# One decode head's attention output: 64 one-column matmuls replaced by 16 wide ones, placed ahead of the V transposes

## The chip, the cores and the metric

The kernel runs on one core of a Trainium2 chip. The metric is the device time of one execution in microseconds (us), the median of several; the profile is of one execution, and its span (first to last instruction) is a little shorter than the device time.

The engines are named as the profile names them: PE is TensorE (matmuls; PEld is its weight loads), DVE is VectorE, ACT is ScalarE, SP is the engine that issues the transfers (DMA).

## The reference

Attention of one query row per head, forward and backward, with B = 1, H = 32 heads, S = 8192 keys, D = 128, all bfloat16:

```python
def _fwd_reference(q, k, v):
    scale = q.shape[-1] ** -0.5
    scores = jnp.einsum('bhqd,bhkd->bhqk', q, k) * scale
    attn = _softmax(scores, axis=-1)
    return jnp.einsum('bhqk,bhkd->bhqd', attn, v)
...
    _out, _vjp = jax.vjp(_f, q, k, v)
    _grads = _vjp(grad_out)
    _out0 = jnp.asarray(_out)
    return (_out0, *[jnp.asarray(_g) for _g in _grads])
```

In the terms of the kernel, for each head, with p the softmax of the scaled scores and do the incoming gradient:

- O = sum over keys of p times the row of V (the output, out_0)
- dV = p times do, an outer product of 8192 x 128 (out_3)
- dp = V times do, and pdt = O times do, one number
- ds = p times (dp - pdt) times the scale
- dQ = sum over keys of ds times the row of K (out_1), and dK = ds times q, an outer product of 8192 x 128 (out_2)

## The kernel before

Each head's K and V are 2 MB each and lie in on-chip memory as [128 partitions, 64 slots, 128], so a partition holds 64 consecutive keys. K has three buffers, V has two, and each of the two outer products has two (`gpool`). Heads go one after another in a written order: a manual schedule, so every engine runs its instructions in the order of the program text, and the program text interleaves head h with the rest of head h - 1.

For one head h the order is:

1. `k_blocks`: VectorE transposes K in 32 x 32 blocks. `k_scores` (L153): 64 matmuls of four columns with the transposed K as weights give the scores. `s_mask` and `s_swap` put them in order.
2. For head h - 1 in between: `ds_of` (L227, L229) forms pdt and ds, `dq_of` (contract, L196) forms dQ with 64 matmuls of one column with K as weights, and `outer(.., "dk", r)` (L206) forms dK in four parts on VectorE.
3. Softmax: the maximum over partitions goes through a TensorE matmul (L273), `rows_bc` spreads the rows of q and do over the partitions, ScalarE takes exp with the row sums (L285), a matmul with ones adds the sums over partitions (L286), VectorE takes the reciprocal `rinv` (L293), and ScalarE writes `p_rep`, the probabilities, each four times side by side, in bf16 (L295).
4. The V stage: `v_transposes(h, c)` for c = 0 to 3, eight f32 transposes each (two bf16 numbers are one f32 word) into a bank pair `T_ps` of which there are two, evicted by ScalarE to `XT_sb` (L179, L181); `v_scores(h, c)`, 16 matmuls of two columns, give dp (L191); `contract(Vt, p_rep)` gives O with 64 matmuls, each with one slot of V as weights and one column of p (L196), which ScalarE copies to a column of `o_all` (L301); a matmul with do spread over columns (L304) gives pdt.
5. `outer(h, "dv", r)`: dV in four parts on VectorE, and its transfer out.

In the V stage before, the two first groups of transposes stand ahead of `contract`, and the rest stands behind it:

```python
        v_transposes(h, 0)
        v_transposes(h, 1)
        contract(Vt[h], x["p"], x["m"][:, 2:3])
        nc.scalar.copy(o_all[:, h:h + 1], x["m"][:, 2:3])
        v_scores(h, 0)
        v_transposes(h, 2)
```

All large transfers go through SP's queue in the order of the text. The load of V for head h + 2 waits until the last transposes of head h have read the buffer; the load of K for head h + 2 waits for `dq_of(h - 1)`. Each PSUM bank used by a head has a name: `s_ps` holds the K scores (one buffer), `dp_ps` holds dp and dQ (two), `m_ps` holds the small results (one): column 0 the sum, column 1 pdt, column 2 O.

Of the kernel before, what the change touches and what calls it, by code (L numbers as in the profile page):

```python
# [12 lines left out]
F32 = mybir.dt.float32  # L13
# [3 lines left out]
R = 4  # L17
# [6 lines left out]
def kernel(  # L24
# [11 lines left out]
    nc = tc.nc  # L36
    P = 128
    _, H, S, D = k.shape
    assert D == P and S % (P * CH) == 0 and H <= P
    NT = S // P  # L40
# [13 lines left out]
    small = ctx.enter_context(tc.tile_pool(name="small", bufs=2))  # L54
# [5 lines left out]
    Kt, Vt, XK, XV, st = {}, {}, {}, {}, {}  # L60

    def rows_of(x, h, c, parts):
        L = NT // parts
        return x[0, h].rearrange("(p n) d -> p n d", p=P)[:, c * L:(c + 1) * L, :]

    def slots(X, c, parts):
        L = NT // parts
        return X[:, c * L:(c + 1) * L, :]
# [23 lines left out]
    ident_f = consts.tile([P, P], F32)  # L92
# [10 lines left out]
    for w in range(NB):  # L103
        for e2 in range(2):
            four = consts.tile([H, NQ, QD], BF16, tag=f"four{w}{e2}")
# [19 lines left out]
    do_f = consts.tile([P, H], F32)  # L125
# [4 lines left out]
    o_all = consts.tile([P, H], F32)  # L130
# [5 lines left out]
    def k_blocks(h, u):  # L136


        if u == 0:
            XK[h] = ktpool.tile([P, CH, NB, NCH, QD], F32, tag="XK", name="XK_sb")  # L140
        nc.vector.transpose(XK[h][:, :, :, u, :],  # L141
                            slots(Kt[h], u, NCH).rearrange("p g d -> p (g d)").bitcast(F32).rearrange(
                                "p (g w j) -> p g w j", g=CH, w=NB))

    def k_scores(h):
        x = st[h]
        x["s"] = psS.tile([P, 512], F32, tag="s", name="s_ps")
        out = x["s"][:, 0:NT].rearrange("p (a g) -> p g a", a=NQ)
        cols = XK.pop(h).rearrange("p g w u i -> p (g w u i)").bitcast(BF16).rearrange(
            "p (g w ui e) -> p g w e ui", g=CH, w=NB, e=2)  # L150
        for g in range(CH):
            for c in range(2 * NB):
                nc.tensor.matmul(out[:, g, :], lhsT=cols[:, g, c // 2, c % 2], rhs=q_blk[:, h, c, :],  # L153
                                 start=(c == 0), stop=(c == 2 * NB - 1), skip_group_check=True)
# [18 lines left out]
    def v_transposes(h, c):  # L173

        T_ps = psT.tile([P, CH // 2, P], F32, tag="T", name="T_ps")
        words = Vt[h].rearrange("p n d -> p (n d)").bitcast(F32)
        for i in range(CH // 2):
            m = c * CH // 2 + i
            nc.tensor.transpose(T_ps[:, i, :], words[:, m * P:(m + 1) * P], ident_f[:])  # L179
        X = tpool.tile([P, CH // 2, P], F32, tag="XT", name="XT_sb")  # L180
        nc.scalar.copy(X[:], T_ps[:])  # L181
        XV[h, c] = X

    def v_scores(h, c):
        X = XV.pop((h, c)).rearrange("p m s -> p (m s)").bitcast(BF16).rearrange("p (m s e) -> p m e s", s=P, e=2)
        if c == 0:
            st[h]["dp"] = psD.tile([P, 512], F32, tag="dp", name="dp_ps")
        for i in range(CH // 2):
            n = c * CH + 2 * i
            for e2 in range(2):  # L190
                nc.tensor.matmul(st[h]["dp"][:, n:n + 2], lhsT=X[:, i, e2, :], rhs=do_blk[:, h, e2, :],  # L191
                                 start=(e2 == 0), stop=(e2 == 1), skip_group_check=True)

    def contract(Xt, rep, out_col, first=0, last=NT):
        for n in range(first, last):
            nc.tensor.matmul(out_col, lhsT=Xt[:, n, :], rhs=rep[:, n, 0:1],  # L196
                             start=(n == 0), stop=(n == NT - 1), skip_group_check=True)

    def outer(h, which, r):
        x = st[h]  # L200
        if r == 0:
            x[which] = gpool.tile([P, NT, D], BF16, tag=which, name="G_" + which)
        G, dst = x[which], out_2 if which == "dk" else out_3
        rep, row = x["ds"] if which == "dk" else x["p"], x["qd"][:, 0 if which == "dk" else 1, :]
        Q = NT // 4
        nc.vector.tensor_tensor(  # L206
            slots(G, r, 4).rearrange("p n (a b) -> p n a b", b=R),
            slots(rep, r, 4).unsqueeze(2).to_broadcast([P, Q, D // R, R]),
            row.rearrange("p (a b) -> p a b", b=R).unsqueeze(1).to_broadcast([P, Q, D // R, R]),
            op=ALU.mult)  # L210
        parts = 4 if h == H - 1 else 2 if h == 0 else 1
        if r % (4 // parts) == 4 // parts - 1:
            c = r // (4 // parts)
            nc.sync.dma_start(rows_of(dst, h, c, parts), slots(G, c, parts))
# [9 lines left out]
    def ds_of(h):  # L224
        x = st[h]
        pdt = small.tile([P, 1], F32, tag="pdt")
        nc.vector.tensor_copy(pdt[:], x["m"][:, 1:2])  # L227
        x["ds"] = small.tile([P, NT, R], BF16, tag="dsrep", name="ds_rep")
        nc.vector.scalar_tensor_tensor(  # L229
            out=x["ds"][:], in0=x["dp"][:, 0:NT].unsqueeze(2).to_broadcast([P, NT, R]), scalar=pdt[:],  # L230
            in1=x["p_s"][:].unsqueeze(2).to_broadcast([P, NT, R]), op0=ALU.subtract, op1=ALU.mult)
# [16 lines left out]
    for h in range(H + 1):  # L248
        p_ = h - 1
        if h < H:  # L250
            x = st[h] = {}
            for u in range(NCH):
                k_blocks(h, u)
            k_scores(h)
        if h > 0:
            ds_of(p_)
            outer(p_, "dk", 0)
            dq_of(p_, 0)
        if h < H:
            s_mask(h)  # L260
            s_swap(h)
        if h > 0:
            dq_of(p_, 1)
            outer(p_, "dk", 1)
        if 0 < h and h + 2 < H:
            load_k(h + 2)
        if h < H:
            mx = small.tile([P, 1], F32, tag="mx")
            nc.vector.reduce_max(mx[:], x["sn"], axis=AX.X)
            diag = small.tile([P, P], F32, tag="diag")  # L270
            nc.vector.tensor_scalar(diag[:], ident_f[:], mx[:], scale, op0=ALU.mult, op1=ALU.mult)
            x["m"] = psM.tile([P, 512], F32, tag="m", name="m_ps")
            nc.tensor.matmul(x["m"][:, 128:256], lhsT=ones_f[:], rhs=diag[:], start=True, stop=True,  # L273
                             skip_group_check=True)
            rows_bc(h)
        if h > 0:
            outer(p_, "dk", 2)
        if h == 0:
            load_k(2)
        if h < H:  # L280
            nbias = small.tile([P, 1], F32, tag="nbias")
            nc.vector.tensor_reduce(nbias[:], x["m"][:, 128:256], axis=AX.X, op=ALU.max, negate=True)  # L282
            e = small.tile([P, NT], F32, tag="e")
            rs = small.tile([P, 1], F32, tag="rs")
            nc.scalar.activation(e[:], x["sn"], ACT.Exp, bias=nbias[:], scale=scale, accum_out=rs[:])  # L285
            nc.tensor.matmul(x["m"][:, 0:1], lhsT=ones_f[:], rhs=rs[:], start=True, stop=True,  # L286
                             skip_group_check=True)
        if h > 0:
            outer(p_, "dk", 3)
        if h == H:  # L290
            break
        rinv = small.tile([P, 1], F32, tag="rinv")
        nc.vector.reciprocal(rinv[:], x["m"][:, 0:1])  # L293
        x["p"] = small.tile([P, NT, R], BF16, tag="prep", name="p_rep")
        nc.scalar.activation(x["p"][:], e[:].unsqueeze(2).to_broadcast([P, NT, R]), ACT.Copy, scale=rinv[:])  # L295
        x["p_s"] = small.tile([P, NT], F32, tag="p_s", name="p_s")
        nc.vector.tensor_scalar(x["p_s"][:], e[:], rinv[:], scale, op0=ALU.mult, op1=ALU.mult)
        v_transposes(h, 0)
        v_transposes(h, 1)
        contract(Vt[h], x["p"], x["m"][:, 2:3])  # L300
        nc.scalar.copy(o_all[:, h:h + 1], x["m"][:, 2:3])  # L301
        v_scores(h, 0)
        v_transposes(h, 2)
        nc.tensor.matmul(x["m"][:, 1:2], lhsT=do_f[:, h:h + 1].to_broadcast([P, P]), rhs=o_all[:, h:h + 1],  # L304
                         start=True, stop=True, skip_group_check=True)
        v_scores(h, 1)
        v_transposes(h, 3)
        v_scores(h, 2)
        v_scores(h, 3)
        outer(h, "dv", 0)  # L310
        outer(h, "dv", 1)
        outer(h, "dv", 2)
        if 0 < h and h + 2 < H:
            load_v(h + 2)
        outer(h, "dv", 3)
        if h == 0:
            load_v(2)
        if h == H - 1:
            result(o_all, out_0)
# [33 lines left out]
```

## Time and profile before

| what | value |
|---|---|
| device time, median of 3 (lowest to highest) | 649.27 us (648.69 to 650.84) |
| span of the profiled execution | 647.3 us |
| mean granted TensorE clock | 0.581 |
| PE / PEld busy | 505.1 us (78%) / 472.7 us (73%) |
| VectorE busy | 513.1 us (79%) |
| ScalarE busy | 183.1 us (28%) |
| bytes moved, mean rate | 269.81 MB, 417 GB/s |
| longest waits: ScalarE's dQ copy for TensorE, ScalarE's V evictions for TensorE, VectorE's dV for an earlier dV transfer | 193.4, 145.8, 66.0 us |

Two engines are busy for nearly four fifths of the span, so busy shares alone don't tell what sets the time. The granted clock is a share of TensorE's full speed. In the slices of the profile a digit is the busy share of one fortieth of the span in tenths, or the clock in tenths; in the chain of waits each piece is named by its start, its length and what ran, and pieces that wait on a transfer carry the transfer's name.

### The profile page before, as it was taken

What the parts mean: (1) busy time and instruction counts of PE and PEld (TensorE: products, weight loads), DVE (VectorE), ACT (ScalarE), POOL (GpSimd) and SP (SyncE); (2) the same over time, 40 slices, a digit from 0 to 9 for tenths busy, and PEclk for the clock granted to TensorE, in tenths of its full rate; (3) what the DMA queues carried; (4) which work ended last, traced back from release to release, by engine and by line L of the source; (5) the groups of instructions that cost most, each with busy time, mean ns of one, the idle gap of its engine ahead of it and who ended that gap; (6) DMA issues with size and microseconds to landing.
All of it is one profiled execution on the core that took longest, in us unless ns stands there. A gap on an engine that the chain in (4) does not pass through costs nothing.

```text
span 647.3 us, 20978 instructions
## 1 busy us (share of the span) xinstructions
PE 505.1 (78%) x9705; PEld 472.7 (73%) x9705; DVE 513.1 (79%) x660; ACT 183.1 (28%) x325; POOL 0.7 (0%) x6
## 2 busy tenths in 40 slices
PE   2888888788968787888768787768887777977970
PEld 1888788688867777878668787668886776877870
DVE  5799889789977779777788777797777977778860
ACT  0333223223333222232222332222322223222240
POOL 0000000000000000000000000000000000000000
PEclk9866555556676555656565565575556666555565
DMA  8999999999999999999999999999999999999984
GB/s 329 413 425 428 424 427 427 426 426 425 428 427 429 426 429 426 431 424 430 425 430 426 431 424 430 430 425 422 426 425 429 427 430 425 427 431 428 409 367 201
DMA packets 20727, 269.81 MB, mean 417 GB/s; under 512 B 2464, under 2 KB 2464, under 8 KB 4512
## 3 DMA queue, kind: packets, MB, share of 16 engines
q1 hardware_dynamic: 20640, 268.48, 97.9%
q8 instruction: 76, 1.25, 0.7%
q14 instruction: 11, 0.09, 0.0%
HBM read 134.23 MB, written 134.23 MB: 415 GB/s over the span
## 4 chain that ended last, share of the span: by engine, by line
DMA 53%; PE 29%; DVE 11%; ACT 3%; issue 1%; SPq 0%; DVEq 0%; ACTq 0%
DMA Kt<-in_k_dram 48%; PE T_ps L179 10%; DVE XK_sb L141 8%; PE s_ps L153 6%; PE dp_ps L196 5%; DMA out_dram<-G_dv 5%; PE m_ps L196 2%; PE dp_ps L191 2%; ACT XT_sb L181 1%; PE s_ps L169 1%; PE m_ps L273 1%; PE m_ps L286 1%; DVE G_dv L206 1%; ACT e L285 1%; ACT qd L222 1%
## 5 line engine op out<-in xcount | busy, mean ns | idle before, releaser
L179 PE MATMUL T_ps<-ident_f,Vt 128*128 128x128 f32 x1024 | 220.4, 396 | 0.0
L206 DVE TENSOR_TENSOR G_dv<-p_rep,qd 128x2048 bf16<-128x2048 bf16 x128 | 148.2, 1221 | 68.5 <-DMA out_dram<-G_dv 66.0
L179 PEld LDWEIGHTS T_ps<-ident_f,Vt 128*128 128x128 f32 x1024 | 195.1, 216 | 0.0
L181 ACT COPY XT_sb<-T_ps 128x1024 f32<-128x1024 f32 x128 | 129.6, 1013 | 145.8 <-PE T_ps L179 145.8
L206 DVE TENSOR_TENSOR G_dk<-ds_rep,qd 128x2048 bf16<-128x2048 bf16 x128 | 155.8, 1219 | 1.1
L141 DVE STREAM_TRANSPOSE XK_sb<-Kt 128x1024 f32<-128x1024 f32 x128 | 148.1, 1214 | 5.6 <-DMA Kt<-in_k_dram 5.5
L153 PE MATMUL s_ps<-q_blk,XK_sb 128*128 128x4 bf16 x2048 | 59.6, 168 | 45.8 <-DVE pdt L227 43.0
L191 PEld LDWEIGHTS <-XT_sb 128*128 128x128 bf16 x2048 | 72.2, 105 | 28.6 <-ACT XT_sb L181 27.0
L191 PE MATMUL dp_ps<-do_blk,XT_sb 128*128 128x2 bf16 x2048 | 73.0, 165 | 24.3 <-ACT XT_sb L181 24.3
L153 PEld LDWEIGHTS <-XK_sb 128*128 128x128 bf16 x2048 | 57.1, 104 | 47.7 <-DVE pdt L227 44.9
L196 PE MATMUL dp_ps<-ds_rep,Kt 128*128 128x1 bf16 x2048 | 64.6, 165 | 3.8 <-issue 3.4
L196 PEld LDWEIGHTS <-Kt 128*128 128x128 bf16 x2048 | 59.8, 104 | 9.5 <-issue 9.4
L196 PEld LDWEIGHTS <-Vt 128*128 128x128 bf16 x2048 | 60.2, 101 | 1.6
L237 ACT COPY dq_all<-dp_ps 128x1 f32<-128x1 f32 x32 | 5.1, 159 | 193.4 <-PE dp_ps L196 193.4
L196 PE MATMUL m_ps<-p_rep,Vt 128*128 128x1 bf16 x2048 | 58.7, 165 | 0.0
L286 PEld LDWEIGHTS m_ps<-rs,ones_f 128*128 128x128 f32 x64 | 16.0, 309 | 48.6 <-ACT e L285 48.6
L286 PE MATMUL m_ps<-rs,ones_f 128*128 128x1 f32 x64 | 18.7, 361 | 39.2 <-ACT e L285 39.2
L273 PE MATMUL m_ps<-diag,ones_f 128*128 128x128 f32 x64 | 25.5, 499 | 2.0 <-issue 1.3
L282 DVE TENSOR_REDUCE nbias<-m_ps 128x1 f32<-128x128 f32 x32 | 9.3, 292 | 21.6 <-ACT qd L222 21.6
L295 ACT ACTIVATE p_rep<-e,rinv 128x256 bf16<-128x256 f32 x32 | 16.3, 508 | 30.3 <-DVE rinv L293 30.3
L222 ACT CAST qd<-m_ps 128x256 bf16<-128x256 f32 x32 | 11.9, 372 | 44.8 <-PE m_ps L218 44.8
L229 DVE SCALAR_TENSOR_TENSOR ds_rep<-dp_ps,pdt,p_s 128x256 bf16<-128x256 f32 x32 | 15.5, 484 | 10.3 <-PE dp_ps L191 8.0
(44 smaller groups left out, 155.1 us busy)
## 6 DMA issues: line engine op xcount, KB each, us to landing
Kt<-in_k_dram SPq DMA_DIRECT2D x31, 2048.0 KB, 30.8
Vt<-in_v_dram SPq DMA_DIRECT2D x31, 2048.0 KB, 28.2
out_dram<-G_dv SPq DMA_DIRECT2D x30, 2048.0 KB, 32.7
out_dram<-G_dk SPq DMA_DIRECT2D x30, 2048.0 KB, 33.0
Kt<-in_k_dram SPq DMA_DIRECT2D x4, 512.0 KB, 5.2
Vt<-in_v_dram SPq DMA_DIRECT2D x4, 512.0 KB, 8.1
out_dram<-G_dv SPq DMA_DIRECT2D x2, 1024.0 KB, 11.0
out_dram<-G_dk SPq DMA_DIRECT2D x2, 1024.0 KB, 12.4
```

The source lines that it names most:

```text
L141: nc.vector.transpose(XK[h][:, :, :, u, :], slots(Kt[h], u, NCH).rearrange("p g d -> p (g d)").bitcast(F32).rearrange("p (g w j) -> p g w ...
L153: nc.tensor.matmul(out[:, g, :], lhsT=cols[:, g, c // 2, c % 2], rhs=q_blk[:, h, c, :], start=(c == 0), stop=(c == 2 * NB - 1), skip_group ...
L179: nc.tensor.transpose(T_ps[:, i, :], words[:, m * P:(m + 1) * P], ident_f[:])
L181: nc.scalar.copy(X[:], T_ps[:])
L191: nc.tensor.matmul(st[h]["dp"][:, n:n + 2], lhsT=X[:, i, e2, :], rhs=do_blk[:, h, e2, :], start=(e2 == 0), stop=(e2 == 1), skip_group_chec ...
L196: nc.tensor.matmul(out_col, lhsT=Xt[:, n, :], rhs=rep[:, n, 0:1], start=(n == 0), stop=(n == NT - 1), skip_group_check=True)
L206: nc.vector.tensor_tensor(slots(G, r, 4).rearrange("p n (a b) -> p n a b", b=R), slots(rep, r, 4).unsqueeze(2).to_broadcast([P, Q, D // R, ...
L222: nc.scalar.copy(x["qd"][:].rearrange("p a d -> p (a d)"), x["m"][:, 256:512])
L229: nc.vector.scalar_tensor_tensor(out=x["ds"][:], in0=x["dp"][:, 0:NT].unsqueeze(2).to_broadcast([P, NT, R]), scalar=pdt[:], in1=x["p_s"][: ...
L273: nc.tensor.matmul(x["m"][:, 128:256], lhsT=ones_f[:], rhs=diag[:], start=True, stop=True, skip_group_check=True)
L286: nc.tensor.matmul(x["m"][:, 0:1], lhsT=ones_f[:], rhs=rs[:], start=True, stop=True, skip_group_check=True)
L295: nc.scalar.activation(x["p"][:], e[:].unsqueeze(2).to_broadcast([P, NT, R]), ACT.Copy, scale=rinv[:])
```

## The change

O is now formed the other way round. The weights are four columns of p (four neighbouring slots of `p_rep`), and the moving operand is 512 columns: the same four slots of V, 128 numbers each. Sixteen such matmuls add up in the bank of the K scores, which is free by then. Of the resulting 4 x 512 numbers only four blocks are wanted: row b with the columns of slot b. ScalarE copies the four rows to `four`, and `gather` adds the diagonal blocks with four small f32 matmuls, each with one block as weights and one column of the identity as the moving operand. O lands in the same column of `m_ps` as before. The number of weight loads of 128 columns falls, and the matmuls with one column go away.

The wide matmuls stand ahead of all V transposes; the gather, ScalarE's copy to `o_all` and the matmul for pdt stand behind the last V scores.

```diff
+    def contract_wide(Xt, rep, bank):
+
+        for g in range(NT // R):
+            nc.tensor.matmul(bank[0:R, :], lhsT=rep[:, R * g:R * (g + 1), 0],
+                             rhs=Xt[:, R * g:R * (g + 1), :].rearrange("p n d -> p (n d)"),
+                             start=(g == 0), stop=(g == NT // R - 1), skip_group_check=True)
+
+    def gather(h):
+        x = st[h]
+        for b in range(R):
+            nc.tensor.matmul(x["m"][:, 2:3], lhsT=x["four"][:, b, :], rhs=ident_f[0:R, b:b + 1],
+                             start=(b == 0), stop=(b == R - 1), skip_group_check=True)
+        nc.scalar.copy(o_all[:, h:h + 1], x["m"][:, 2:3])
+        nc.tensor.matmul(x["m"][:, 1:2], lhsT=do_f[:, h:h + 1].to_broadcast([P, P]), rhs=o_all[:, h:h + 1],
+                         start=True, stop=True, skip_group_check=True)
...
+        contract_wide(Vt[h], x["p"], x["s"])
         v_transposes(h, 0)
         v_transposes(h, 1)
-        contract(Vt[h], x["p"], x["m"][:, 2:3])
-        nc.scalar.copy(o_all[:, h:h + 1], x["m"][:, 2:3])
+        x["four"] = small.tile([R, R, D], F32, tag="four", name="four")
+        nc.scalar.copy(x["four"][:].rearrange("a b d -> a (b d)"), x["s"][0:R, :])
         v_scores(h, 0)
         v_transposes(h, 2)
-        nc.tensor.matmul(x["m"][:, 1:2], lhsT=do_f[:, h:h + 1].to_broadcast([P, P]), rhs=o_all[:, h:h + 1],
-                         start=True, stop=True, skip_group_check=True)
         v_scores(h, 1)
         v_transposes(h, 3)
         v_scores(h, 2)
         v_scores(h, 3)
+        gather(h)
         outer(h, "dv", 0)
```

## The prediction

> **What bounds the kernel now.** I read the page's slices first, then the chain of waits in order of time, then the timeline and the busy windows of one head.
>
> ```profile
> PEclk9866555556676555656565565575556666555565
> GB/s 329 413 425 428 424 427 427 426 426 425 428 427 429 426 429 426 431 424 430 425 430 426 431 424 430 430 425 422 426 425 429 427 430 425 427 431 428 409 367 201
> ```
>
> The transfers run flat at about 427 GB/s. A head moves 8.39 MB (K and V in, dK and dV out), so the queue needs 19.7 us per head. The chain agrees: two heads lie between these two starts of the K scores, and a K load ends the wait between them.
>
> ```profile
> 391.16 1.87 PE s_ps L153 x64
> ...
> 395.23 30.85 DMA Kt<-in_k_dram
> ...
> 430.78 1.87 PE s_ps L153 x64
> ```
>
> 39.62 us for two heads is 19.81 us each. How far below that is the arithmetic? In the first heads buffers are still free and the chain stays on the engines:
>
> ```profile
> 101.01 1.71 PE s_ps L153 x64
> 102.72 0.85 PE dp_ps L196 x32
> 103.94 0.94 PE dp_ps L196 x32
> 104.88 0.74 PE m_ps L273 x2
> 106.71 0.41 ACT e L285 x2
> 107.17 0.58 PE m_ps L286 x2
> 107.75 3.52 PE T_ps L179 x16
> 111.27 1.60 PE m_ps L196 x64
> 113.26 0.94 PE T_ps L179 x8
> 114.72 1.77 PE T_ps L179 x8
> 116.57 1.02 ACT XT_sb L181
> 117.64 0.58 PE dp_ps L191 x16
> 118.22 1.71 PE s_ps L153 x64
> ```
>
> One head is 17.21 us: 6.16 us from the K scores to the softmax sum (L286), then 11.05 us of V stage. The slack under the transfers is only 19.81 - 17.21 = 2.6 us, and TensorE sets the 17.21. VectorE is busy 15.8 us of that, so it's not the first bound. A change may add 2.6 us to the V stage for nothing; each further us costs about 31 us over the heads.
>
> The first V transposes also cover the way to the probabilities, as the timeline shows:
>
> ```profile
> 107.79 0.17 DVE L293 RECIPROCAL rinv<-m_ps 128x1 f32<-128x1 f32 x1
> 108.05 0.51 ACT L295 ACTIVATE p_rep<-e,rinv 128x256 bf16<-128x256 f32 x1 [0.94 <-DVE rinv L293]
> 134.08 0.55 PEld L304 LDWEIGHTS m_ps<-o_all,do_f 128*128 128x128 f32 x2
> ```
>
> p_rep is ready at 108.56, 1.4 us after L286 began, while TensorE transposes. The clock decides what streaming costs:
>
> ```profile
> 110.50:111.00 0.50, 0.50 (x4) 0.50 (x3) 0.50 (x2) 0.11 (x1) 0.00 (x0) 0.50 1.07 459
> 111.00:111.50 0.50, 0.50 (x18) 0.44 (x16) 0.50 (x1) 0.20 (x1) 0.00 (x0) 0.75 1.07 459
> 111.50:112.00 0.50, 0.50 (x27) 0.50 (x24) 0.50 (x1) 0.50 (x1) 0.00 (x0) 1.00 0.92 393
> 114.50:115.00 0.50, 0.50 (x12) 0.50 (x10) 0.50 (x1) 0.50 (x1) 0.00 (x0) 0.66 0.84 360
> ```
>
> The granted clock is 0.5 except for stretches of about 3.4 us (here 111.25 to 114.66). At 0.5 a transpose takes 0.22 us (3.52/16), at full clock 0.117 (0.94/8). The contraction takes 25 ns per matmul at either clock.
>
> **What the Trainium skill says.** "TensorE: Matmul & The Clock Gate", section "What's actually happening": the clock is half unless an activity window of about 3.4 us, free-running, was busy. The trace agrees: the rises at 111.25, 165.86 and 203.4 lie a whole number of 3.413 us steps apart. The window filled by transposes (107.84 to 111.25) raised the clock. One with 2.3 us of them (128.3 to 131.7) didn't; nor did the full stretch of 4-column and 1-column matmuls from 101.0 to 104.4. So streamed columns count, and more than two thirds of a window is wanted. The same page, "Weight-path perf modes", says that non-FP32 loads of 128 weights are fast: the trace has 104 ns recorded for bf16 against 216 to 310 for f32, and the 64 pairs pace at 25 ns. So the old form was cheap: it moved one column per load.
>
> **The change part by part**, per head, from the start of L286.
> - *Removed:* the contraction, 64 x 25 ns = 1.60 us, and the 0.12 to 0.55 us of L304 between transposes.
> - *Moved ahead, a new wait:* the wide matmuls need p_rep, so TensorE waits until 108.56 + 0.04, 1.43 us after L286 began. L286 itself fills 0.58; 0.85 is idle. All transposes and V scores are queued behind.
> - *Added, 16 matmuls of 512 moving columns.* No row of the trace has one. The skill's page prices them, in "Wait — 56ns, not 53.3ns?", at 426.7 ns cold and 215.7 warm: 6.83 or 3.45 us in all. Their 4-column loads hide behind the streams, as the transposes' loads do now. I take the wide matmuls to count as activity. With the window's edge anywhere, in three of four heads the clock rises one full window after the first edge (2.56 to 5.97 us later than the start becomes 3.41 to 5.97, mean 4.69), in the fourth at the first edge (mean 2.99): 4.27 us on average. Cold until then, warm after: 4.27 + (6.83 - 4.27)/2 = 5.55 us.
> - *V transposes and scores behind it:* the rest of the wide stream and 16 transposes fill the next window, so the clock stays up. Then ScalarE sets the pace: first 8 transposes 0.94, four evictions of 1.01 each with hand-overs 4.2, the new copy of four rows in their midst partly shown 0.6, last V scores 0.6: 6.35 us. The copy is priced by "ScalarE: Activation LUTs", "What ACT_TABLE_LOAD costs": 186 + 0.833 x 512 = 612 ns (the same formula gives 1039 for the 1024-column eviction that takes 1013 here). All cold it would be 3.52 + 0.43 + 1.81 + 0.43 + 1.81 + 1.05 + 0.6 = 9.65 us.
> - *Gather:* four f32 matmuls of one column, each with two f32 loads. L304 is the nearest row: 0.55 us cold for two loads, 0.30 at full clock; in a queue 0.43 each. 4 x 0.43 + 0.15 = 1.87; ScalarE's o_all copy 0.16 with hand-overs 0.25; then L304, 0.58. Sum 2.7 us cold, 1.5 warm. V scores have left the clock to fall, so 2.7. Before, o_all's copy lay beside transposes; now the next K scores (L153) stand behind it on TensorE.
> - *pdt and ds_rep* (VectorE) come after L304 and so start as the K scores do: the mask is pushed by about 0.25 us.
>
> V stage: 1.43 + 5.55 + 6.35 + 2.7 = 16.03 us in place of 11.05. Head: 6.16 + 0.25 + 16.03 = 22.44, and 0.3 for pauses in issue (the seven early heads have 1.33 + 2.04 us of them, 0.48 a head; TensorE has 18% fewer instruction rows now). That is 22.74 us, above 19.81: TensorE becomes the bound and the transfers fall to 8.39 MB / 22.74 us = 369 GB/s. VectorE's 15.8 us stays beside it. No load arrives late: a K load gets some 30 us before its transposes, and those have 6 us to spare.
>
> Total: first L286 at 19.0 as now; 31 x 22.74 = 704.9; last V stage 16.0; ds and dK 5.4; last transfer, with no queue before it, about 4; and 1.75 us between span and time: 751 us.
>
> **The rivals.**
> *A. The wide stream doesn't count as activity* (only 4 of 128 weight columns are used): 1.43 + 6.83 + 9.65 + 2.7 = 20.6, a head of 27.3, in all 19 + 31 x 27.3 + 20.6 + 11.2 = 897 us. For it: 4-column matmuls never raised the clock. Against it: those had idle columns in time; this stream has none.
> *B. The wide matmuls pace faster than a column per cycle.* The same skill page gives 131 ns per 512 columns in a sustained stream ("Back-to-back issue gap"), at odds with its other figure. Then 2.1 us; 1.43 + 2.1 + 7.5 (transposes half cold) + 2.7 = 13.7; a head of 20.4; about 675 us.
> *C. Hidden, not slower:* all at full clock: 1.43 + 3.45 + 6.35 + 1.5 = 12.7, a head of 19.4, under the transfers' 19.81: 649 us. Against it: the clock must be up before the stream begins, after an idle stretch.
> *D. Faster:* the transfers would have to begin earlier or be fewer. The last reader of V is still the last transpose; nothing speaks for it.
>
> **How the numbers follow.** Forecast 0.73, A 0.12, B 0.08, C 0.05, D 0.02. The forecast's own spread comes from the gather (1.5 to 2.7) and the clock after the wide part (6.35 to 9.0 us for the transposes): heads of 21.5 to 25.4 us, 712 to 838. B is taken in, A and C are left out: 670 to 840. Faster 0.02, same 0.05, slower 0.93.
>
> **What would show it.** The chain should leave the K loads and stay on TensorE, with the K scores about 22.7 us apart in every stage and DMA below nine tenths; wide matmuls at 0.43 then 0.22 us with the clock rising inside them; 1.4 us from L286's start to the first of them; transposes behind at 0.117; gather and its copy 2.7 us before the K scores. A K load on the chain at 19.8 us per head would prove me wrong; wide matmuls all at 0.43 would be A.

## The result, and the profile after

The changed kernel takes 728.39 us (median of 4, 725.60 to 731.33), the kernel before 649.37 us beside it: a ratio of 1.121 (95% interval 1.116 to 1.127). It is 79 us slower. The prediction said 751 us, between 670 and 840.

The page of the changed kernel: its slices of clock, of the DMA engines' busy share and of the transfer rate, the shares of the chain of waits, then the costliest group and one row of the transfers (last column: us from issue to landing):

```profile
PEclk9976677776777777677767777776777677777767
DMA  8989899999999999999999999999999999999954
GB/s 322 427 307 394 323 362 385 382 388 376 376 376 416 388 397 373 397 376 383 417 393 375 382 393 373 371 393 366 357 352 397 389 370 378 399 385 395 397 211 171
...
PE 60%; DVE 20%; ACT 14%; issue 4%; DMA 1%; SPq 0%; DVEq 0%; ACTq 0%
...
L202 PE MATMUL s_ps<-Vt,p_rep 128*4 128x512 bf16 x512 | 182.0, 534 | 27.8 <-ACT p_rep L311 27.8
...
Kt<-in_k_dram SPq DMA_DIRECT2D x31, 2048.0 KB, 13.2
```

The rate is no longer flat at 427: it wanders about 380 GB/s, and a K load lands after 13.2 us where it took 30.8. Transfers hold 1% of the chain, where they held 53% in the kernel before. The queue is waiting for the engines now. The clock is higher than before (0.742 on average against 0.581), so a busier and faster TensorE goes with a slower kernel.

The chain of waits of one head of the changed kernel (start, length, what ran):

```profile
306.38 6.40 PE s_ps L202 x16
312.78 1.04 PE T_ps L179 x8
...
313.84 1.02 ACT XT_sb L181
...
314.91 0.56 PE dp_ps L191 x16
315.46 0.93 PE T_ps L179 x8
316.40 0.38 PE dp_ps L191 x16
316.78 0.95 PE T_ps L179 x8
...
317.80 1.02 ACT XT_sb L181
...
318.87 0.55 PE dp_ps L191 x16
319.42 0.99 PE m_ps L209 x8
...
320.44 0.17 ACT o_all L211
...
320.65 0.40 PE m_ps L212 x2
...
321.07 0.17 DVE pdt L243
...
328.76 5.46 PE s_ps L202 x16
```

No transfer stands between the two streams, 22.4 us apart. The stream took 6.40 us here and 5.46 in the next head. The transposes behind it run at 0.12 us each, and the gather (L209), ScalarE's copy and the pdt matmul (L212) stand bare before pdt on VectorE. From pdt on the chain runs mostly through VectorE (ds and the parts of dK), and the next stream starts 7.7 us after pdt; in this head the K scores run beside that and don't set the time.

Why do two equal streams differ? The busy windows of the first of these heads (PE, PEld, DVE, ACT, POOL busy, then the clock, then the DMA share and GB/s):

```profile
308.30:311.00 2.70, 2.70 (x7) 0.76 (x6) 2.70 (x4) 0.00 (x0) 0.00 (x0) 0.50 1.02 434
311.00:312.20 1.20, 1.20 (x5) 0.39 (x4) 1.20 (x2) 0.00 (x0) 0.00 (x0) 0.56 1.02 437
312.20:313.00 0.80, 0.80 (x6) 0.36 (x5) 0.80 (x1) 0.00 (x0) 0.00 (x0) 1.00 1.01 430
...
319.60:320.50 0.90, 0.80 (x8) 0.71 (x7) 0.00 (x0) 0.06 (x1) 0.00 (x0) 1.00 0.99 364
```

The stream began at 306.38 at half clock; the clock rose at 312.05, shortly before the end. In other heads the rise comes earlier. It then stays up through the gather.

### The profile page after: what moved, and what is told of

It is laid out like the page before. It is cut to its first block, busy times and chain, and to the rows that moved or that the text cites. A ratio compares the mean times of both kernels' runs of the same rounds, so it can differ in the third digit from the quotient of the medians.

```text
span 728.3 us, 18386 instructions
## 1 busy us (share of the span) xinstructions
PE 585.4 (80%) x8425; PEld 415.6 (57%) x8425; DVE 512.4 (70%) x660; ACT 194.5 (27%) x357; POOL 0.7 (0%) x6
## 3 DMA queue, kind: packets, MB, share of 16 engines
q1 hardware_dynamic: 20640, 268.48, 93.8%
## 4 chain that ended last, share of the span: by engine, by line
PE 60%; DVE 20%; ACT 14%; issue 4%; DMA 1%; SPq 0%; DVEq 0%; ACTq 0%
PE s_ps L202 25%; PE T_ps L179 13%; DVE G_dk L222 13%; ACT XT_sb L181 9%; PE dp_ps L191 7%; PE m_ps L209 4%; PE m_ps L289 3%; ACT p_rep L311 2%; PE dp_ps L196 2%; PE s_ps L153 2%; PE m_ps L212 2%; ACT qd L238 2%; DVE ds_rep L245 2%; PE m_ps L234 1%; DVE nbias L298 1%
## 5 line engine op out<-in xcount | busy, mean ns | idle before, releaser
L202 PE MATMUL s_ps<-Vt,p_rep 128*4 128x512 bf16 x512 | 182.0, 534 | 27.8 <-ACT p_rep L311 27.8
L181 ACT COPY XT_sb<-T_ps 128x1024 f32<-128x1024 f32 x128 | 126.6, 1015 | 236.0 <-PE T_ps L179 236.0
L202 PEld LDWEIGHTS <-p_rep 128*4 128x4 bf16 x512 | 53.9, 110 | 142.5 <-issue 96.5
L179 PE MATMUL T_ps<-ident_f,Vt 128*128 128x128 f32 x1024 | 131.5, 276 | 0.0
L179 PEld LDWEIGHTS T_ps<-ident_f,Vt 128*128 128x128 f32 x1024 | 110.2, 141 | 14.0 <-issue 14.0
L243 DVE COPY pdt<-m_ps 128x1 f32<-128x1 f32 x32 | 5.1, 158 | 159.9 <-PE m_ps L212 159.9
L191 PE MATMUL dp_ps<-do_blk,XT_sb 128*128 128x2 bf16 x2048 | 70.1, 164 | 32.7 <-ACT XT_sb L181 32.7
L191 PEld LDWEIGHTS <-XT_sb 128*128 128x128 bf16 x2048 | 63.4, 97 | 44.2 <-ACT XT_sb L181 42.9
L302 PE MATMUL m_ps<-rs,ones_f 128*128 128x1 f32 x64 | 18.9, 363 | 40.4 <-ACT e L301 39.2
L302 PEld LDWEIGHTS m_ps<-rs,ones_f 128*128 128x128 f32 x64 | 16.1, 310 | 49.8 <-ACT e L301 48.5
L209 PE MATMUL m_ps<-ident_f,four 4*128 4x1 f32 x256 | 33.5, 248 | 0.0
L209 PEld LDWEIGHTS m_ps<-ident_f,four 4*128 4x128 f32 x256 | 30.8, 186 | 0.6
## 6 DMA issues: line engine op xcount, KB each, us to landing
Kt<-in_k_dram SPq DMA_DIRECT2D x31, 2048.0 KB, 13.2
```

The lines of the kernel that those rows point to most:

```text
L202: nc.tensor.matmul(bank[0:R, :], lhsT=rep[:, R * g:R * (g + 1), 0], rhs=Xt[:, R * g:R * (g + 1), :].rearrange("p n d -> p (n d)"), start=( ...
L209: nc.tensor.matmul(x["m"][:, 2:3], lhsT=x["four"][:, b, :], rhs=ident_f[0:R, b:b + 1], start=(b == 0), stop=(b == R - 1), skip_group_check ...
```

## The experiments

Averages over heads 1 to 30, read from TensorE's timeline of each run, in us. "V" is from the start of the softmax sum (L286 before, L302 after) to the end of the last V scores; "gap" from there to the next K scores, be it for the gather or for VectorE and a K load; "rest" from the K scores to the next softmax sum.

| run | time | to first wide | V | gap | rest | head |
|---|---|---|---|---|---|---|
| before | 649 | - | 11.45 | 1.41 | 6.48 | 19.34 |
| after | 728.4 | 1.50 | 13.79 | 1.49 | 6.71 | 22.00 |
| e1_narrow_ahead | 656.5 | - | 11.54 | 1.56 | 6.43 | 19.53 |
| e2_two_of_16 | 647.8 | 1.45 | 10.39 | 2.44 | 6.44 | 19.27 |
| e3_wide_behind_two | 685.1 | 4.03 | 12.56 | 1.57 | 6.77 | 20.90 |
| e4_gather_earlier | 690.7 | 1.50 | 13.96 | 0.09 | 6.77 | 20.82 |
| e5_both_moves | 661.6 | 3.95 | 12.64 | 0.13 | 6.92 | 19.69 |
| s1_one_more | 682.7 | - | 13.84 | -0.12 | 6.89 | 20.61 |
| s2_two_more | 781.5 | - | 16.80 | -0.13 | 6.89 | 23.55 |
| s3_half_more | 659.5 | - | 12.69 | 0.06 | 6.93 | 19.68 |
| n1_narrow_tail | 648.9 | - | 11.10 | 1.78 | 6.45 | 19.33 |
| c1_four_strips | 645.5 | 3.97 | 9.87 | 2.78 | 6.60 | 19.25 |
| c2_strips_only | 651.7 | 1.46 | 10.92 | 1.90 | 6.48 | 19.31 |

Small negative gaps are overlaps in TensorE's pipeline. The profiled execution of e3 took 692.3 us, 7 us more than the median of its three others, which the table gives, so the rest of its row is about 0.2 us a head too long.

The transfer rate in GB/s by stretch of the span, for some of these runs:

| run | 20 to 100 us | 150 to 450 us | 450 us to 60 us before the end | last 60 us |
|---|---|---|---|---|
| before | 423 | 428 | 427 | 346 |
| after | 364 | 389 | 378 | 269 |
| e1_narrow_ahead | 412 | 427 | 427 | 311 |
| e5_both_moves | 393 | 427 | 423 | 321 |
| s3_half_more | 400 | 427 | 424 | 313 |
| n1_narrow_tail | 423 | 427 | 428 | 345 |

### The order alone: the old contraction ahead of all transposes

```diff
-        v_transposes(h, 0)
-        v_transposes(h, 1)
         contract(Vt[h], x["p"], x["m"][:, 2:3])
+        v_transposes(h, 0)
+        v_transposes(h, 1)
```

> The old 64-matmul contraction alone is moved ahead of all V transposes; its copy and the pdt matmul stay where they were. Slack theory (the head has about 2.6 us under the transfers, and only what exceeds it shows): the wait for p_rep leaves 0.85 us idle and the clock is raised less often, a head of about 19 us, still under 19.8, so 649 to 655 us and K loads still on the chain. Rival (the exposed wait for p_rep and the order are what costs): clearly slower, 665 us or more.

656.49 us, ratio 1.011 (1.010 to 1.013): 7 us, a little more than the slack theory's end and far from the rival's. V hardly grew (11.54 for 11.45), since the transposes ran at a higher clock: their weight loads sum to 166.1 us against 195.1. I had written that the clock would be raised less often; it was raised more often (0.666 on average, 0.581 before). K loads are still on the chain. The 7 us lie at the two ends of the run: from 150 us to the last 60 us the transfers run at 427 to 428 GB/s in both kernels, but from 20 to 100 us they reach 412 GB/s in place of 423, and in the last 60 us 311 in place of 346. At 427 GB/s that is 2 and 5 us of transfers. So the move costs nothing where the transfers set the time. Which step of the last heads makes them later isn't shown.

### The stream cut to two of sixteen

This kernel leaves out 14 of the 16 slices of the sum for O, and pdt, dQ and dK follow from that O.

```diff
-        for g in range(NT // R):
+        for g in (0, NT // R - 1):
```

> The changed kernel with the first and the last of the 16 wide matmuls alone: it leaves out 14 sixteenths of the sum in O, and all that depends on O. Clock theory (the stream's cost is partly paid back, since it raises the clock for the transposes, V scores and gather behind it): the stage behind runs at half clock again, 9 to 10 us in place of 6.5 and a gather of 2 to 2.7 us in place of 1.6, so a head of 20.5 to 21 us and 670 to 710 us. Rival (costs simply add up, 5.6 us of stream gone down to 0.86): a head of about 17 us, hidden under the transfers, 649 us.

647.82 us, ratio 0.998 (0.997 to 0.999). By its time the rival won. The trace shows that neither was right. Part of its chain:

```profile
300.44 3.61 PE T_ps L179 x16
304.04 0.40 PE dp_ps L191 x16
304.45 1.53 PE T_ps L179 x8
305.98 0.38 PE dp_ps L191 x16
306.36 0.95 PE T_ps L179 x8
...
309.01 1.80 PE m_ps L209 x8
```

The first sixteen transposes are back at 0.225 us each, as I expected, and the gather at 1.80 us, a little under the 2 to 2.7 expected. But the transposes raise the clock without the stream: it rose at 305.57, and the 3.41 us before that held transposes and V scores alone. So the later transposes run at 0.12. From the first transpose to the last V scores it is 7.99 us on average, against 6.71 behind the whole stream: the stream pays back 1.3 us of its 5.6, not 3 and not nothing. With 4.6 us of stream gone and 1.3 lost, the engines' head falls under the transfers.

### The stream behind two groups of transposes

```diff
-        contract_wide(Vt[h], x["p"], x["s"])
         v_transposes(h, 0)
         v_transposes(h, 1)
+        contract_wide(Vt[h], x["p"], x["s"])
```

> The wide matmuls stand where the old contraction stood, behind the first two groups of transposes; the gather stays at the end. Clock theory: the transposes start at once and bring the clock up for the stream, which then takes about 3.8 us; V stage about 13.8 us in place of 15.1, head near 20.4, 660 to 690 us. Rival (the stream costs 5.6 us wherever it stands and only the 0.85 us of idle time is won): about 700 us or more.

685.14 us, ratio 1.055 (1.051 to 1.058), within the clock theory's numbers and below the rival's. V fell by 1.23 us, which is more than the 0.85 us of idle time: the transposes bring the clock up early in the stream. It rises 1.0 us after the first wide matmul on average, where it took 4.2, and the stream takes 4.1 us in place of 5.6.

### The gather ahead of the last V scores

```diff
-        v_scores(h, 3)
         gather(h)
+        v_scores(h, 3)
+        pdt_of(h)
```

(`pdt_of` is the last matmul of `gather`, split off.)

> The changed kernel with the four gather matmuls and ScalarE's o_all copy ahead of the last V scores, where TensorE waits for the last eviction; the pdt matmul stays at the end. If the gather's whole stretch is exposed now (1.6 us a head), 0.8 to 1.0 us of it is hidden: 695 to 705 us. Rival (something else, such as VectorE's or ScalarE's queue, ends at the same time): unchanged, 725 us or more.

690.67 us, ratio 1.064 (1.061 to 1.068): 38 us won, 1.2 us a head, somewhat more than the 0.8 to 1.0 I expected. The gap fell from 1.49 to 0.09 us, V grew by 0.17. Nearly all of the gather hides in the wait for the last eviction.

### Both moves

The diffs of the two runs above, together.

> Both moves: wide matmuls behind the first two groups of transposes, gather ahead of the last V scores. Slack theory: the gains add up to a head of about 19.5 us, at the transfers' pace: 649 to 665 us, K loads on the chain again; it can't be faster than the kernel before, since the bytes are the same. Rival (the wide form itself can't fit under the transfers): 680 us or more.

661.58 us, ratio 1.019 (1.016 to 1.021). The time is in the slack theory's range, but K loads did not come back to the chain (1% of it), as that theory had expected. Singly the moves won 43 and 38 us; together they win 67, and it stays 12 us behind the kernel before. From 150 to 450 us the transfers run at 427 GB/s again. Most of the 12 us are lost at the ends: 393 GB/s from 20 to 100 us and 321 in the last 60 us, where the kernel before has 423 and 346.

### A ruler for the slack

```diff
         contract(Vt[h], x["p"], x["m"][:, 2:3])
+        contract(Vt[h], x["p"], x["m"][:, 3:4])
```

and once more into column 4, and with 32 matmuls only.

> A ruler for the slack: the kernel before with its contraction of V done twice (the second into a column that nobody reads), 1.6 us more of TensorE per head. Slack theory: a head of about 18.8 us of engine work, hidden: 649 to 653 us. Rival (any added TensorE work shows): 1.6 x 31 = 50 us more, 699 us.

> The same ruler with the contraction done three times, 3.2 us more per head. Slack theory: 17.2 + 3.2 = 20.4 us, past 19.8: 660 to 680 us. Rival (transfers alone set the time): 649 us; rival (any added work shows): 748 us.

> A finer step of the ruler: the kernel before with half a contraction more (32 one-column matmuls into a column that nobody reads, 0.8 us). If the slack is what the heads with the clock down leave (12.2 us of V stage + 6.3 us, 18.5 us of 19.8), a head of 19.3 us and some pauses is hidden: 649 to 655 us. Rival (no slack at all; the 33 us of the 1.6 us step are in proportion): 665 us.

682.67 us (ratio 1.052, 1.050 to 1.054), 781.49 (1.203, 1.197 to 1.208) and 659.53 (1.016, 1.014 to 1.018), for 1.6, 3.2 and 0.8 us of added matmuls. All three are worse than the slack theory said, the second also than the rival that counts every added us (748); the first and the third stay below their rivals (699 and 665). TensorE's waits in the run with two more contractions, in order of their sum (us, times, longest):

```profile
PE m_ps L286 <- ACT e L285: 39.2, 32, 1.2
PE m_ps L196 <- issue: 25.4, 13, 2.7
PE dp_ps L191 <- ACT XT_sb L181: 24.2, 32, 0.8
PE dp_ps L191 <- issue: 10.5, 7, 2.3
PE dp_ps L196 <- issue: 9.1, 4, 2.6
```

The rows of "issue" are pauses in which TensorE waited for no other engine: 47.1 us with those of the transposes, against 4.7 in the kernel before. The pages' rows of instruction loads, before and with two more contractions (packets, MB, share of the DMA engines):

```profile
q8 instruction: 76, 1.25, 0.7%
...
q8 instruction: 108, 1.77, 0.9%
```

That is one packet of 16 KB for each 256 of TensorE's instructions, matmuls and weight loads (2 x 9,705 before, 2 x 13,801 here). Each of the 27 pauses of this run ended 2.2 to 2.5 us after such a packet had begun. The longest began at 568.49 us, a packet at 568.80, and TensorE went on at 571.23. So TensorE stood waiting for its own instructions. The pauses don't grow in proportion to what is added: 14.9 us with half a contraction more, 14.6 with one, 47.1 with two. The second part is the clock: with one more contraction the transposes' weight loads sum to 209.1 us (195.1 before), with two more to 211.0. In V, 0.8 us of added matmuls cost 1.24 us, 1.6 cost 2.39, 3.2 cost 5.35.

Where was the slack, then? Before, the engines' own head is V 11.45 - 0.14 + rest 6.48 = 17.8 us on average, not the 17.2 of the one head I read, which had the clock raised; the first nine heads, which waited for no K load, took 17.9. And the limit is not 19.81 but (616.34 - 19.01)/31 = 19.27 us, the mean over all heads from the first softmax sum to the last: the first heads run ahead of the transfers while buffers are free. The slack is about 1.5 us, and a change that draws pauses or loses clock uses more of it than its own time: with 0.8 us added, V grew by 1.24 us and the rest of the head by 0.45.

### The old contraction, pdt at the end

```diff
-        nc.scalar.copy(o_all[:, h:h + 1], x["m"][:, 2:3])
...
         v_scores(h, 3)
+        nc.scalar.copy(o_all[:, h:h + 1], x["m"][:, 2:3])
+        nc.tensor.matmul(x["m"][:, 1:2], lhsT=do_f[:, h:h + 1].to_broadcast([P, P]), rhs=o_all[:, h:h + 1],
+                         start=True, stop=True, skip_group_check=True)
```

> The kernel before with the old contraction in its old place, and only the o_all copy and the pdt matmul moved behind the last V scores, as in the changed kernel. With nothing to gather, the copy is done before TensorE comes there, and about 0.4 us of matmul is all that is exposed: 649 to 653 us. Rival (the place behind the last scores is itself what delays pdt, ds and the next head by 1.5 us): 665 us or more.

648.89 us, ratio 1.000 (0.999 to 1.001). This kernel has slack in which a cost could hide, but its rates in the first 100 us and in the last 60, where e1's loss showed, are those of the kernel before too. So the place behind the last scores costs nothing that shows; what costs in the changed kernel is the four gather matmuls and the copy that must wait for them.

### Four strips side by side

```diff
-            nc.tensor.matmul(bank[0:R, :], lhsT=rep[:, R * g:R * (g + 1), 0],
+            j, w = g % 4, g // 2
+            nc.tensor.matmul(bank[j * QD:(j + 1) * QD, :],
+                             lhsT=rep[:, 8 * w:8 * (w + 1), :].rearrange("p n r -> p (n r)"),
                              rhs=Xt[:, R * g:R * (g + 1), :].rearrange("p n d -> p (n d)"),
-                             start=(g == 0), stop=(g == NT // R - 1), skip_group_check=True)
+                             start=(g < 4), stop=(g >= NT // R - 4), skip_group_check=True)
```

A strip is 32 rows of the output. The copy then takes all 128 rows, and the gather's moving operand is a column of `sel`, a constant that holds ones in the four rows with block b and zeros elsewhere. First with both moves, then in the change's own order.

> As the version with both moves, but the 16 wide matmuls go in turn to four strips of 32 output partitions, with 32 columns of weights each (eight slots of p_rep, of which four matter), and the gather picks its rows with a constant of zeros and ones. If matmuls in different strips run side by side, four take the time of one, about 0.43 us at half clock, the 16 about 1.7 to 2 us in place of 3.7, and the head falls well under the transfers' pace: 649 to 653 us. Rival (they run one after another all the same): 3.7 us and about 661 us as before.

> The changed kernel, order and all, with only the four strips: wide matmuls ahead of all transposes, gather at the end. If the serial stream is what costs most of the 79 us, its 5.6 us become about 1.8, the stage behind goes to about 8 us as with two of the sixteen (the clock is up for less of it), the gather stretch stays at 1.5 to 2.4: a head of 19 to 19.7 us, 649 to 660 us. Rival (the order, with its bare wait for p_rep and the gather at the end, costs as much as the stream): 680 us or more.

645.53 us, ratio 0.994 (0.993 to 0.996), 3 us less than the kernel before and below the 649 to 653 expected; and 651.71, ratio 1.005 (1.003 to 1.006), as expected. Two streams of the first, from its timeline:

```profile
300.99 1.90 PE L209 MATMUL s_ps<-Vt,p_rep 128*32 128x512 bf16 x16
320.56 1.05 PE L209 MATMUL s_ps<-Vt,p_rep 128*32 128x512 bf16 x16
```

and the clock in each:

```profile
301.00:301.80 0.80, 0.80 (x9) 0.28 (x12) 0.80 (x1) 0.71 (x1) 0.00 (x0) 0.50 0.91 389
320.60:321.50 0.90, 0.90 (x17) 0.29 (x16) 0.76 (x1) 0.83 (x1) 0.00 (x0) 1.00 1.09 455
```

Sixteen matmuls of 512 columns take 1.90 us at half clock and 1.05 at full, so four do run beside each other. The Trainium skill describes this in "TensorE: Matmul & The Clock Gate", "Part 3: Packing small matmuls — row/col tiling": outputs in different strips of 32 partitions run at once, 2.38 times as fast with three strips. Against the 6.83 us that sixteen matmuls at half clock, 0.427 us each, take one after another, four strips are 3.6 times as fast here. In the change's own order that alone takes away 77 of the 79 us. So the length of the serial stream is enough to explain nearly all of the loss: the order and the gather, at full price in the trace, find room under the transfers once it is short. It isn't the only cost that will do. With the serial stream kept, the two moves took away 67 us. The costs follow one another on one path: a head has to lose about 2.7 us (22.0 to 19.3), from whichever of them, to be back at the pace of the kernel before.

## Why the prediction was right

- *TensorE becomes the bound.* Shown by the chain without transfers and the fallen rate. The mean head is 22.00 us, 22.74 was said. One sign named beforehand did not come: the DMA engines' busy share stays at nine tenths in most slices (93.8% for the large transfers, 97.9% before), though the rate fell from 427 to about 380 GB/s. Only the rate shows that the transfers wait.
- *The wait for p_rep:* 1.43 us said, 1.50 on average (1.44 in most heads).
- *The stream:* 5.55 us said; V 13.79 - 1.50 - 6.71 = 5.58 on average, at 0.427 us and then about 0.215 each. The clock rises 2.67 to 5.94 us into the stream, 4.16 on average; 4.27 was said, from the assumption that 2.56 us of stream in a window raise it. A window with 2.67 us of stream did, and one with 2.53 (5.94 - 3.41) did not. Rival A, that four columns of weights don't count as activity, fell: the clock rises inside the stream. Rival B, 131 ns per 512 columns in one strip, fell too: nothing in this trace is near that.
- *Transposes and scores behind it:* 6.35 us said, 6.71 measured. ScalarE doesn't set the pace throughout: in the head shown above it waits 0.21 and 0.35 us for the third and the fourth group of transposes, which I had left out. The copy of four rows took 0.57.
- *The gather* was the mis-sized term: 2.7 us said with the clock fallen, a gap of 1.49 measured with it up. My 1.5 at full clock was the right end. The step that failed is "V scores have left the clock to fall": in each of the 32 heads the clock stays up for 10.24 us, three windows of 3.41, and so through the gather. In the head shown above the window with the third and fourth group (315.47 to 318.88) held 1.9 us of transposes and the clock stayed up behind it, where 2.3 us in a window did not raise it in the kernel before. Why less is enough to keep it up than to raise it stays open; no run tests it. 1.2 us in 31 heads is 37 us too much; the 0.36 us above and 0.07 of longer wait give 13 back. That is about the 23 us between 751 and 728.
- *Mask and pauses:* 6.16 + 0.25 + 0.3 said for the rest of the head, 6.71 measured: 6.43 in most heads, more where there are pauses. The instruction rows of TensorE fell by 13% (9,705 to 8,425), not by the 18% that stands beside this term.
- *The slack of 2.6 us* was wrong, and the forecast was right in spite of it: its total rests on the engines' own head, so the size of the slack didn't enter. The ruler puts it at 1.5 us or less. Had the change added 2 us a head, I would have called it hidden and been wrong, as I was for the 1.6 us of the ruler.

Read at its core: in the V stage one contraction of 1.6 us became 5.6 us of stream, and TensorE starts on V 1.05 us later (1.50 us after the softmax sum begins, 0.45 before). Transposes and V scores, now mostly at full clock, give back 2.7 us (6.71 us, where they took 11.02 - 1.60 = 9.42). That leaves V 2.3 us longer. The 1.5 us of gather come on top; they stand where the kernel before waited 1.4 us for a K load.

## What to carry to other kernels

A weight load of 128 columns with one moving column costs 25 ns in a queue here, so fewer, wider matmuls aren't cheaper as such: count the moving columns, 64 x 25 ns against 16 x 512 columns. If the wide form uses few weight columns, put its outputs in four strips of 32 partitions so that four streams run at once. And read slack from the mean of many heads on both sides of the comparison, with the clock and the pauses in it, not from the best head. Look at the first and last heads apart: a change that is hidden at the transfers' pace can still cost there (7 us in the run with the old contraction ahead).

## What I hadn't expected of the hardware

- In the V stage added one-column matmuls cost more than their time: 0.8, 1.6 and 3.2 us a head lengthened it by 1.24, 2.39 and 5.35 us, and the kernel by 10.6, 33.5 and 132 us. The clock is raised less, and TensorE waits for its own instructions: all 120 pauses "issue" in the thirteen traces end 2.2 to 2.6 us after a 16 KB packet of instructions began.
- Four matmuls of 512 columns into four strips took 0.475 us together at half clock (1.90/4); one alone takes 0.427.
- A slower kernel can have the higher clock: 0.742 on average at 728 us, 0.581 at 649 us.
